# The first token group's attention in one fixed order, with value sums and key copies on GpSimd

## The chip, the cores and the metric

One core of one Trainium2 chip runs the whole kernel. The metric is the device time of one execution in microseconds (us), the median of three runs; a profile of one further execution stands beside it. Engines are named as in the profile: PE is TensorE (PEld its weight loads), DVE VectorE, ACT ScalarE, POOL GpSimd, SP the engine that issues most DMAs.

## What is computed

Three stages in a row: attention with keys and values averaged over 8 neighbours, a softplus feed-forward layer, and a layer of 8 experts of which each token takes one.

```python
def _attn_ref(q, k, v):                # 8 batches, 8 heads, 576 tokens, 64 wide
    k_p = k.reshape(B, H, Sp, pool, D).mean(axis=3)      # pool = 8, Sp = 72
    v_p = v.reshape(B, H, Sp, pool, D).mean(axis=3)
    scores = scale * np.matmul(q, k_p.transpose(0, 1, 3, 2))
    scores = scores - np.max(scores, axis=-1, keepdims=True)
    attn = np.exp(scores)
    attn = attn / (np.sum(attn, axis=-1, keepdims=True) + 1e-09)
    return np.matmul(attn, v_p)

def _moe_ref(x, w_in, w_out):          # x is 4608 x 512, w_in 512 x 2048, w_out 2048 x 512
    h = x @ w_in
    g = np.maximum(h, 0.0) + np.log1p(np.exp(-np.abs(h)))
    return g @ w_out
...
```

`w_in` and `w_out` arrive as 64-bit floats. The third stage, the experts, is not touched by the change.

## The kernel before

**Groups and blocks.** The 4608 tokens are worked on in nine groups of 512 (`g`). A group's attention has four units (`hp`, two heads each). Unit `u` needs its keys `kT[u]`, queries and values `vT[u]`, each with 128 partitions (two heads of 64). Groups and batches do not line up (512 against 576 tokens): the first group needs the keys and values `u` = 0 to 3, the second group these and `u` = 4 to 7.

**The first group's unit** (`unit0`, L576 to L617) takes these steps. DVE sums each eight keys (`keys`, L531), ACT copies the sum into the two halves of a block-diagonal tile `kbd` (L538, L539; there are two such tiles, used in turn), PE makes the scores `s` (L586), DVE subtracts the largest (L594, L595), ACT takes the exponential (L543), DVE sums, adds, inverts (L544 to L546), POOL multiplies (L547). For the values PE does eight accumulating products `pv` with the identity (L604), which sum and transpose at once; ACT copies the result (`vp`, L606). PE transposes the shares (`tr`, L613), ACT copies them (L614), PE makes the output `o` (L570). ACT writes its rounded part `xh` (L572) and DVE the remainder `xl` (L573). The steps stand in a generator; `Feed.tick` advances all units that are open by one step, and one step of the weights follows each tick.

**The second group's unit** (`unit`, L619 to L669) does the same in other tiles; there DVE sums keys and values by a reduction (L531, L554), and one transpose (L561) turns the value sum.

**The weights** (`load_weights`, L464) come as 64-bit words. A piece is loaded (`raw`), ACT unpacks it in two instructions (L470, L472), DVE joins the parts in two (L475, L477), ACT writes the rounded part `wh` (L492, L520) and DVE the remainder `wl` (L494, L521). The first four column blocks come in six halves of 512 words ("early halves"), through three small buffers in `boot2`; the other twelve in whole blocks of 1024 words, two to a tile (`raw2` to `raw7`, `wt2` to `wt7`).

**The feed-forward layer.** For block `c` of 16, `p1` makes 12 products h (L716), ACT and DVE do the softplus (L722 to L729) and leave `gh` and `gl`; `p2` makes 12 products y (L740 to L742) two blocks later. `p1` of block c needs tile `wt[c // 2]`. The first group's 16 blocks need the weights as they come; later groups find them all there. Between the blocks, ticks of `Feed` run the next group's attention.

**What sets the order.** A scheduler places the instructions: each engine's list is in the order that its plan gives, not the order of the code; after that each engine works its list strictly from the front.

Of the kernel before, what the change touches and what calls it, by code (L numbers as in the profile page):

```python
# [15 lines left out]
ALU = mybir.AluOpType  # L16
# [20 lines left out]
def tile_kernel(ctx, tc, qT, kT, vT, wbits, w9, w1, w2, out):  # L37
# [383 lines left out]
    with ExitStack() as ph:  # L421
# [37 lines left out]
        STEPS = 6 * EARLY + 6 * (8 - EARLY // 2)  # L459
# [4 lines left out]
        def load_weights():  # L464
# [15 lines left out]
            def half(c, j, first):  # L480
# [8 lines left out]
                unpack(lo, hi)  # L489
# [10 lines left out]
            for c in range(EARLY):  # L500
                for j in range(2 if c >= LAG else 1):
                    yield from half(c, j, True)
            for i in range(EARLY // 2, 8):
# [5 lines left out]
                for j in range(2):  # L509
                    lo, hi = raw[:, j, :, 0], raw[:, j, :, 1]  # L510
                    unpack(lo, hi)
# [15 lines left out]
        count = [0]  # L527
        def keys(u, k, kv):
# [37 lines left out]
        def output(us, et, hp, xh, xl, ps=ps_a, tag="pa"):  # L566
            o = ps.tile([P, 512], F32, tag=tag, name="o")
# [4 lines left out]
            nc.scalar.activation(out=xh[:, hp, :], in_=o, func=AF.Copy, scale=0.125)  # L572
            nc.vector.scalar_tensor_tensor(out=xl[:, hp, :], in0=o, scalar=0.125,  # L573
                                           in1=xh[:, hp, :].bitcast(F32), op0=ALU.mult, op1=ALU.subtract)

        def unit0(hp, us, xh, xl, g):  # L576
            (u, r0, rn, c0), = us
            q, k = room("q", G, True), room("kv", 576, True)
            nc.sync.dma_start(out=k, in_=kT[u])
            nc.sync.dma_start(out=q, in_=qT[u, :, r0:r0 + rn])  # L580
            yield
            yield
            banks = [ps_y.tile([P, 512], F32, tag=f"y{hp % 2 * 2 + i}", name="s") for i in range(2)]
            kb = keys(u, k, lambda: room("kv", 576, True))
            for t in range(T):
                nc.tensor.matmul(banks[t // 3][:, t % 3 * 144:(t % 3 + 1) * 144],  # L586
                                 lhsT=q[:, t * P:(t + 1) * P], rhs=kb, start=True, stop=True)
            e = k.rearrange("p (a k) -> p a k", k=SP)
            st = room("st", 24, True)
# [198 lines left out]
        for i, it in enumerate(feed.units):  # L788
            next(it)
            if i:  # L790
                weights(1)
# [225 lines left out]
```

## Time and profile before

| | us |
|---|---|
| three runs | 1360.51, 1362.04, 1363.5 |
| median | 1362.04 |
| the profiled execution | 1360.56 |
| its span, first to last instruction | 1358.8 |
| PE busy in the span | 1330.1 (98%) |
| DVE, ACT, POOL busy | 847.6, 595.0, 308.0 |

The span is the time between the first and the last instruction on the core; the execution's time has 1.8 us more around it. Busy time of PE counts a product from its start to its modelled end. The share over the whole span hides that the stages differ: the first 35 us are the first group's attention, the stretch to some 130 us is the first group's feed-forward layer with the unpacking of the weights beside it, then come eight groups with all weights there, then the experts. Everything that the change moves lies in the first 130 us.

### The profile page before, as it was taken

To read this page: it belongs to the slowest core of one execution; us is meant where nothing else is said; L and a number is where in the kernel's file an instruction comes from. 1 tells how busy PE (TensorE), PEld (TensorE's weight loads), DVE (VectorE), ACT (ScalarE), POOL (GpSimd) and SP (SyncE) were. 2 spreads that over 40 slices of the span, in tenths; PEclk is the share of its full clock that TensorE was granted. 3 is DMA by queue.
4 is the path that set the end of the run, shared out by engine and by line. 5 is a ranking of instruction groups with operands and counts; after the bars stand their busy time and mean duration, and the time that the engine had idled before them with its cause. 6 is when DMAs were issued, how large, how long until landed. Compare 5 with 4: busy or idle time off the path is not lost. (4 is left out here: it accounts for less than half of the span.)

```text
span 1358.8 us, 21365 instructions
## 1 busy us (share of the span) xinstructions
PE 1330.1 (98%) x7030; PEld 1110.0 (82%) x7030; DVE 847.6 (62%) x1951; ACT 595.0 (44%) x1076; POOL 308.0 (23%) x375
## 2 busy tenths in 40 slices
PE   6999999999999999999999999999999999999996
PEld 5777787778878778778778778889989898989885
DVE  7998794974974964965946847545655332326263
ACT  6996544544555445545455444551111111114152
POOL 2010111121021030030130120343233343233334
PEclk9999999999999999999999999999999999999998
DMA  7642432241341340431421301503322222243363
GB/s 274 256 150 79 125 106 68 77 126 35 83 128 29 99 125 17 119 102 31 119 70 28 111 14 46 196 23 94 96 79 95 71 63 75 69 136 112 123 212 88
DMA packets 149743, 134.17 MB, mean 99 GB/s; under 512 B 100933, under 2 KB 116933, under 8 KB 147056
## 3 DMA queue, kind: packets, MB, share of 16 engines
q1 hardware_dynamic: 131744, 95.51, 24.3%
q0 software_dynamic: 17872, 37.13, 8.6%
q8 instruction: 60, 0.98, 0.3%
q14 instruction: 67, 0.55, 0.1%
HBM read 168.77 MB, written 29.67 MB: 146 GB/s over the span
## 5 line engine op out<-in xcount | busy, mean ns | idle before, releaser
L716 PE MATMUL h<-xh,wt 128*128 128x512 f32 x1152 | 379.7, 390 | 0.3 <-DVE xl L573 0.3
L716 PEld LDWEIGHTS h<-xh,wt 128*128 128x128 f32 x1152 | 216.2, 188 | 46.0 <-DVE xl L573 1.2
L740 PE MATMUL y<-wt,gh 128*128 128x512 f32 x576 | 232.8, 404 | 0.0
L894 PE MATMUL h<-xt,w1h 128*128 128x256 f32 x1280 | 226.4, 281 | 2.7 <-PEq L918 2.0
L120 DVE CUSTOM_DVE_ANT_0 junk<-rows,w9b 128x512 bf16<-128x512 f32 x324 | 222.4, 686 | 8.1 <-ACT rows L114 3.2
L741 PE MATMUL y<-wt,gh 128*128 128x512 f32 x576 | 225.2, 391 | 0.0
L742 PE MATMUL y<-wt,gl 128*128 128x512 f32 x576 | 225.1, 391 | 0.0
L716 PE MATMUL h<-xl,wt 128*128 128x512 f32 x576 | 224.7, 390 | 0.0
L894 PEld LDWEIGHTS h<-xt,w1h 128*128 128x128 f32 x1280 | 196.4, 188 | 5.1 <-issue 2.8
L894 PE MATMUL h<-xt,w1l 128*128 128x256 f32 x640 | 179.5, 280 | 0.7 <-DVEq L962 0.7
L898 ACT ACTIVATE hs<-h 128x512 fp32r<-128x512 f32 x80 | 47.7, 598 | 301.5 <-PE h L894 180.3
L722 ACT ACTIVATE a<-h 128x512 f32<-128x512 f32 x144 | 85.8, 596 | 175.8 <-PE h L716 169.7
L725 DVE SCALAR_TENSOR_TENSOR a<-h,a 128x512 f32<-128x512 f32 x144 | 98.5, 684 | 102.8 <-ACT a L724 102.2
L727 ACT ACTIVATE gh<-a 128x512 fp32r<-128x512 f32 x144 | 90.8, 631 | 160.6 <-DVE a L725 158.2
L740 PEld LDWEIGHTS y<-wt,gh 128*128 128x128 f32 x576 | 108.1, 188 | 35.2 <-ACT a L722 7.7
L742 PEld LDWEIGHTS y<-wt,gl 128*128 128x128 f32 x576 | 108.2, 188 | 25.5 <-issue 2.1
L716 PEld LDWEIGHTS h<-xl,wt 128*128 128x128 f32 x576 | 108.2, 188 | 22.3 <-issue 0.2
L741 PEld LDWEIGHTS y<-wt,gh 128*128 128x128 f32 x576 | 108.3, 188 | 20.0 <-issue 0.2
L729 DVE TENSOR_TENSOR gl<-a,gh 128x512 fp32r<-128x512 f32 x144 | 101.0, 701 | 37.6 <-ACT gh L727 34.9
L894 PEld LDWEIGHTS h<-xt,w1l 128*128 128x128 f32 x640 | 122.1, 191 | 0.9 <-DVEq L962 0.9
L928 DVE SCALAR_TENSOR_TENSOR ys<-y,xg 128x512 f32<-128x512 f32 x38 | 28.5, 750 | 145.3 <-PE y L926 115.8
L926 PE MATMUL y<-w2h,hs 128*128 128x512 f32 x304 | 118.5, 390 | 0.6 <-DVE hs L899 0.6
(198 smaller groups left out, 1815.0 us busy)
## 6 DMA issues: line engine op xcount, KB each, us to landing
w9b<-w SPq DMA_DIRECT2D x81, 256.0 KB
raw<-wbits SPq DMA_DIRECT2D x12, 1024.0 KB
x2d<-rows SPq DMA_DIRECT2D x36, 260.0 KB
et<-q SPq DMA_DIRECT2D x256, 32.0 KB
kv<-vT SPq DMA_DIRECT2D x28, 288.0 KB
kv<-kT SPq DMA_DIRECT2D x24, 288.0 KB
xm<-misc SPq DMA_DIRECT2D x160, 32.0 KB
misc<-misc SPq DMA_DIRECT2D x144, 32.0 KB
```

The costliest lines, as they stand in the source:

```text
L120: nc.vector.tensor_tensor_reduce(out=ws["junk"], in0=rows[t][:, :D], in1=w9b[e], scale=1.0, scalar=0.0, op0=ALU.mult, op1=ALU.add, accum_o ...
L716: nc.tensor.matmul(h, lhsT=l, rhs=r[:, kk, :], start=n == 0, stop=n == 11)
L722: nc.scalar.activation(out=a, in_=h, func=AF.Abs)
L725: nc.vector.scalar_tensor_tensor(out=a, in0=h, scalar=0.0, in1=a, op0=ALU.max, op1=ALU.add)
L727: nc.scalar.activation(out=gh, in_=a, func=AF.Copy)
L729: nc.vector.tensor_tensor(out=gl, in0=a, in1=gh.bitcast(F32), op=ALU.subtract)
L740: nc.tensor.matmul(y, lhsT=th, rhs=wh, start=c == 0, stop=False)
L741: nc.tensor.matmul(y, lhsT=th, rhs=wl, start=False, stop=False)
L742: nc.tensor.matmul(y, lhsT=tl, rhs=wh, start=False, stop=c == 15)
L894: nc.tensor.matmul(h[:, f2, :], lhsT=l, rhs=r[:, kk, :], start=n == 0, stop=n == 11)
L898: nc.scalar.activation(out=hh[:, fs, :], in_=h, func=AF.Relu)
L926: nc.tensor.matmul(y, lhsT=hl[:, f, js], rhs=ws["w2h"][:, f, :], start=False, stop=f == 7)
```

## The change

**The first group.** `unit0` becomes a class whose steps are methods, and `lead_in` calls the steps of the four units in one written order. `in_order` then ties each instruction that is issued inside it to the one before it on the same engine, DMA issues on SP included, so that the plan keeps this order; other instructions may still stand between. The key sum stays on DVE; its two copies into `kbd` go from ACT to POOL. The value sum goes from PE (eight products) to POOL (three adds, `add8`), and PE does one transpose of it (`values`). All value loads are issued ahead of the first weights. Units 2 and 3 take other PSUM banks for values and outputs.

**The second group.** Its key and value sums (`u` = 4 to 7) go from DVE to POOL (`pool8`); the copies into `kbd` stay on ACT.

**The weights.** An early half's load is issued two halves ahead of its unpacking. Some instructions are held behind others (`after`): unpackings of the third and later early halves, and of the first large blocks, behind the first group's rounding on ACT; the first two blocks of `p1` behind the first group's transposes on PE; the second group's first maximum behind the first group's remainders on DVE; the first second-group key sum behind the first group's adds on POOL.

```diff
...
+            its = [half(c, j, True) for c in range(EARLY) for j in range(2 if c >= LAG else 1)]
+            for n in range(2):
+                next(its[n])
+                yield
+            for n, it in enumerate(its):
+                if n + 2 < len(its):
+                    next(its[n + 2])
+                yield from it
...
+        def after(eng, cond=True):
+            return tc.issue_after(behind[eng]) if cond else nullcontext()
...
-                nc.vector.tensor_reduce(kp, k.rearrange("p (s w) -> p s w", w=8), AX.X, ALU.add)
+                pool8(kp, k, u)
...
-                    nc.vector.tensor_reduce(vr, v.rearrange("p (s w) -> p s w", w=8), AX.X, ALU.add)
+                    pool8(vr, v, u)
...
-            for w in range(8):
-                nc.tensor.matmul(pv[:SP, :P], lhsT=v8[:, w], rhs=ident, start=w == 0, stop=w == 7)
...
+            for ins in traced[start:]:
+                if ins.engine in prev:
+                    tc.add_manual_dep(ins, prev[ins.engine].name,
+                                      mybir.DependencyInfo(mybir.DependencyClass.NoSync, mybir.DependencyReason.DATA),
+                                      reason="in_order")
+                prev[ins.engine] = ins
...
+        def add8(out, t):
+            t3 = t.rearrange("p (s w) -> p s w", w=8)
+            for n in (4, 2):
+                nc.gpsimd.tensor_tensor(out=t3[:, :, :n], in0=t3[:, :, :n], in1=t3[:, :, n:2 * n], op=ALU.add)
+            behind["POOL"] = nc.gpsimd.tensor_tensor(out=out.unsqueeze(2), in0=t3[:, :, 0:1], in1=t3[:, :, 1:2],
+                                                     op=ALU.add).ins
...
+        def pool8(out, t, u):
+            if u < 8:
+                with after("POOL", u == 4):
+                    add8(out, t)
+            else:
+                nc.vector.tensor_reduce(out, t.rearrange("p (s w) -> p s w", w=8), AX.X, ALU.add)
...
+                nc.gpsimd.tensor_copy(self.kb[0:64, 0:SP], kp[0:64, :])
+                nc.gpsimd.tensor_copy(self.kb[64:128, SP:2 * SP], kp[64:128, :])
...
+            def vsum(self):
+                add8(self.vr, self.v)
...
-        while feed.units or jobs:
-            feed.tick()
+        def lead_in():
+            u0, u1, u2, u3 = us = units_of(0)
+            for u in us:
+                u.load_v()
+            weights(2)
+            u0.key()
+            u0.score()
+            u1.key()
+            u1.score()
+            u0.top()
+            u2.key()
+            u0.exp()
+            u0.share()
+            u2.score()
+            u0.vsum()
+            u1.top()
+            u1.exp()
+            u3.key()
+            u1.share()
+            u0.value()
+            u0.turned()
+            u3.score()
...
+        with in_order():
+            lead_in()
...
```

**Places where it moves instructions.** ACT at the end of the first group's attention, up to the first softplus instruction (`a`). `boot_170<-tr` are the turned shares, `boot2_171` the early halves, `kbd` the key tiles, `o` and `xh` the outputs and their rounding; `raw2` and `raw3` are the large loads. Before:

```order
L614 ACTIVATE boot_170<-tr_381 72x512
L614 ACTIVATE boot_170<-tr_387 72x512
L572 ACTIVATE xh_175<-o_396 128x512
L470 ACTIVATE boot2_171<-boot2_171 128x512
L472 ACTIVATE boot2_171<-boot2_171 128x512
L572 ACTIVATE xh_175<-o_402 128x512
L472 ACTIVATE raw2_450<-raw2_450 128x1024
L470 ACTIVATE raw2_450<-raw2_450 128x1024
L492 ACTIVATE wt1_182<-boot2_171 128x512
L722 ACTIVATE a_425<-h_412 128x512
```

The same place now:

```order
L577 ACTIVATE vp_348<-pv_346 72x128
L552 ACTIVATE kbd1_167<-kp_455 64x72
L684 ACTIVATE boot_170<-tr_350 72x512
L684 ACTIVATE boot_170<-tr_356 72x512
L470 ACTIVATE boot2_171<-boot2_171 128x512
L472 ACTIVATE boot2_171<-boot2_171 128x512
L587 ACTIVATE xh_175<-o_365 128x512
L553 ACTIVATE kbd1_167<-kp_455 64x72
L552 ACTIVATE kbd0_165<-kp_203 64x72
L553 ACTIVATE kbd0_165<-kp_203 64x72
L495 ACTIVATE wt0_189<-boot2_171 128x512
L587 ACTIVATE xh_175<-o_373 128x512
```

Before, the sixth early half's rounding (`wt1`) stands just ahead of the first softplus instruction, and a large load is partly unpacked; now only the second half's (`wt0`) is done, and a key copy of the second group (`kp_455`, summed on POOL) stands ahead of the last turned shares.

POOL in the same stretch had four multiplies (L547) in a row and then the second group's. Now its list between the multiplies (L668) of units 0 and 1, and from those of units 2 and 3 to the second group's first key sum, is:

```order
L668 TENSOR_TENSOR boot_kv_169<-boot_kv_169,boot2_171 128x576
L610 TENSOR_TENSOR boot_kv_169<-boot_kv_169 128x72x4
L610 TENSOR_TENSOR boot_kv_169<-boot_kv_169 128x72x2
L611 TENSOR_TENSOR boot2_171<-boot_kv_169 128x72
L643 COPY kbd1_167<-kp_240 64x72
L644 COPY kbd1_167<-kp_240 64x72
L668 TENSOR_TENSOR boot_kv_169<-boot_kv_169,boot2_171 128x576
```

```order
L668 TENSOR_TENSOR boot_kv_169<-boot_kv_169,boot2_171 128x576 x2
L610 TENSOR_TENSOR boot2_171<-boot2_171 128x72x4
L610 TENSOR_TENSOR boot2_171<-boot2_171 128x72x2
L611 TENSOR_TENSOR boot2_171<-boot2_171 128x72
L610 TENSOR_TENSOR kk_412<-kk_412 128x72x4
L610 TENSOR_TENSOR kk_412<-kk_412 128x72x2
L611 TENSOR_TENSOR kp_455<-kk_412 128x72
```

Each value sum has come in as three rows behind a multiply, and the second group's key sum (`kp_455`) stands behind unit 3's value sum.

ACT ahead of the first write of a weight tile that comes from a large load. Before, `wt2` is written after the rounding of one block's softplus:

```order
L470 ACTIVATE raw3_516<-raw3_516 128x1024
L727 ACTIVATE gh_430<-a_425 128x512
L724 ACTIVATE a_468<-a_468 128x512
L520 ACTIVATE wt2_511<-v_477 128x1024
L520 ACTIVATE wt2_511<-v_482 128x1024
```

Now:

```order
L495 ACTIVATE wt1_190<-boot2_171 128x512
L806 ACTIVATE a_576<-h_563 128x512
L470 ACTIVATE raw3_585<-raw3_585 128x1024
L807 ACTIVATE a_576<-a_576 128x512
L472 ACTIVATE raw3_585<-raw3_585 128x1024
L808 ACTIVATE a_576<-a_576 128x512
L470 ACTIVATE raw3_585<-raw3_585 128x1024
L529 ACTIVATE wt2_535<-v_511 128x1024
```

The write now stands behind the softplus of the fourth block (`h_563`, c = 3), where before it stood behind the second block's.

## Rows read from the trace of the kernel before

**Rows 1.** Busy us (count): PE, PEld, DVE, ACT, POOL; clock, DMA share, GB/s.

```profile
24.00:95.00 71.00, 68.69 (x335) 52.31 (x334) 65.93 (x94) 69.00 (x111) 7.29 (x7) 1.00 0.62 228
```

**Rows 2.** Waits of PE, 35.4 to 130 us: total, times, longest.

```profile
PE s L636 <- ACT kbd L539: 1.4, 2, 1.2
PE pv L561 <- DVE vr L554: 0.5, 1, 0.5
```

**Rows 3.** Timeline of PE: start, us, line, out<-in, shape, count, [idle before].

```profile
5.22 2.29 PE L586 MATMUL s<-kbd,boot 128*128 128x144 f32 x8 [5.22 <-ACT kbd L539]
...
19.25 1.15 PE L586 MATMUL s<-kbd,boot 128*128 128x144 f32 x8
...
20.45 2.33 PE L604 MATMUL pv<-ident,boot_kv 128*72 128x128 f32 x16
...
26.73 1.08 PE L570 MATMUL o<-boot,vp 72*64 72x512 f32 x4
...
35.41 0.50 PE L716 MATMUL h<-xh,wt 128*128 128x512 f32 x1 [0.32 <-DVE xl L573]
...
42.40 1.39 PE L636 MATMUL s<-kbd,q 128*64 128x144 f32 x8 [1.22 <-ACT kbd L539]
...
54.52 0.39 PE L716 MATMUL h<-xh,wt 128*128 128x512 f32 x1
...
60.40 0.27 PE L561 MATMUL pv<-ident,vr 128*72 128x128 f32 x1 [0.50 <-DVE vr L554]
...
93.95 0.61 PE L716 MATMUL h<-xh,wt 128*128 128x512 f32 x2
```

**Rows 4.** Timeline of DVE.

```profile
3.84 0.75 DVE L531 TENSOR_REDUCE kp<-boot_kv 128x72 f32<-128x576 f32 x1 [2.54 <-DMA boot_kv<-kT]
...
17.98 0.20 DVE L546 RECIPROCAL boot<-boot 128x8 f32<-128x8 f32 x1
18.61 1.40 DVE L494 TENSOR_TENSOR wt<-boot,wt 128x512 fp32r<-128x512 f32 x1 [0.43 <-ACT wt L492]
...
22.38 0.69 DVE L477 SCALAR_TENSOR_TENSOR boot<-boot 128x512 int32<-128x512 int32 x1
22.99 0.75 DVE L544 TENSOR_REDUCE boot<-boot_kv 128x8 f32<-128x576 f32 x1
...
46.54 1.21 DVE L521 TENSOR_TENSOR wt<-v,wt 128x1024 fp32r<-128x1024 f32 x1
```

**Rows 5.** Timeline of ACT.

```profile
4.62 0.26 ACT L538 ACTIVATE kbd<-kp 64x72 f32<-64x72 f32 x1 [2.54 <-DVE kp L531]
...
22.99 0.67 ACT L470 ACTIVATE boot<-boot 128x512 f32<-128x512 f32 x1
...
24.12 0.66 ACT L492 ACTIVATE wt<-boot 128x512 fp32r<-128x512 f32 x1
24.68 1.06 ACT L614 ACTIVATE boot<-tr 72x512 f32<-72x512 f32 x2
...
46.90 0.61 ACT L727 ACTIVATE gh<-a 128x512 fp32r<-128x512 f32 x1
47.42 0.57 ACT L722 ACTIVATE a<-h 128x512 f32<-128x512 f32 x1
47.90 0.67 ACT L543 ACTIVATE q<-q 128x576 f32<-128x576 f32 x1
48.47 0.61 ACT L723 ACTIVATE a<-a 128x512 f32<-128x512 f32 x1
48.99 1.14 ACT L472 ACTIVATE raw<-raw 128x1024 int32<-128x1024 uint32 x1
50.03 0.61 ACT L724 ACTIVATE a<-a 128x512 f32<-128x512 f32 x1
```

**Rows 6.** Timeline of POOL.

```profile
18.32 1.15 POOL L547 TENSOR_TENSOR boot_kv<-boot_kv,boot 128x576 f32<-128x576 f32 x1 [3.06 <-DVE boot L546]
...
43.86 0.26 POOL L649 MEMSET q<- 128x192 f32 x1 [12.33 <-PE s L636]
```

More of the change, by code (lines that the diff above doesn't have):

```diff
@@ L488, in half @@
                 lo, hi = raw[:, :, 0], raw[:, :, 1]
-                unpack(lo, hi)
+                if first:
+                    yield
+                with after("ACT", first and c > 1):
+                    unpack(lo, hi)
                 yield
@@ L510, in load_weights @@
                     lo, hi = raw[:, j, :, 0], raw[:, j, :, 1]
-                    unpack(lo, hi)
+                    with after("ACT", i < 4):
+                        unpack(lo, hi)
                     yield
@@ new lines, in round_x, with rest_x, in_order @@
+        def round_x(o, hp, xh):
+            return nc.scalar.activation(out=xh[:, hp, :], in_=o, func=AF.Copy, scale=0.125)
+        def rest_x(o, hp, xh, xl):
+            return nc.vector.scalar_tensor_tensor(out=xl[:, hp, :], in0=o, scalar=0.125,
+                                                  in1=xh[:, hp, :].bitcast(F32), op0=ALU.mult, op1=ALU.subtract)
+        @contextmanager
+        def in_order():
+            traced = nc.cur_bb.bb.instructions
+            mark = traced[-1]
+            yield
+            start = next(k for k in reversed(range(len(traced))) if traced[k] is mark) + 1
+            prev = {}
+            for ins in traced[start:]:
[4 more added lines that the diff above has]
+                prev[ins.engine] = ins
@@ L644, in unit @@
                 m = mx[:, 4 * b:4 * b + 4].rearrange("p (t h) -> p t h", t=2)
-                nc.vector.tensor_reduce(m, s4, AX.X, ALU.max)
+                with after("DVE", g == 1 and hp == 0):
+                    nc.vector.tensor_reduce(m, s4, AX.X, ALU.max)
                 nc.vector.tensor_tensor(out=e4[:, 2 * b:2 * b + 2, :, :SP], in0=s4, op=ALU.subtract,
@@ L668, in unit @@
             yield
-            output(us, et.rearrange("p (a k) -> p a k", a=2)[:SP], hp, xh, xl)
+            o = ps_a.tile([P, 512], F32, tag="pa", name="o")
+            attend(o, us, et.rearrange("p (a k) -> p a k", a=2)[:SP])
+            round_x(o, hp, xh)
+            rest_x(o, hp, xh, xl)
         X = {}
@@ L682, in units_of @@
                 t0 += n
-            return [(unit if g else unit0)(hp, [(b * 4 + hp, *r) for b, *r in part], xh, xl, g) for hp in range(4)]
+            return [unit(hp, [(b * 4 + hp, *r) for b, *r in part], xh, xl, g) if g else
+                    Unit0(hp, [(b * 4 + hp, *r) for b, *r in part], xh, xl) for hp in range(4)]
         jobs, ends = [], []
@@ L785, in last_group @@
                 split2()
-        feed.start(units_of(0), 1)
[L788 to L791, printed above, removed]
-        while feed.units or jobs:
-            feed.tick()
-            weights(1)
+        def lead_in():
[20 more added lines that the diff above has]
+            u3.score()
+            u2.top()
+            u2.exp()
+            u1.vsum()
+            u0.product()
+            u0.high()
+            u3.top()
+            u2.vsum()
+            u2.share()
+            u1.value()
+            u1.turned()
+            u3.exp()
+            u3.share()
+            weights(1)
+            u1.product()
+            u1.high()
+            u3.vsum()
+            weights(1)
+            u0.low()
+            u1.low()
+            u2.value()
+            u2.turned()
+            weights(1)
+            u3.value()
+            u3.turned()
+            weights(1)
+            u2.product()
+            u2.high()
+            u2.low()
+            weights(1)
+            u3.product()
+            u3.high()
+            weights(1)
+            u3.low()
+        with in_order():
+            lead_in()
         pend = []
```

124 lines of the change are left out of this document (69 added, 55 removed).

## Prediction

> **What bounds the kernel now.** I read the busy table of the stretch behind the first group's attention first, then TensorE's waits, then each engine's rows in the lead-in. From 24 to 95 us TensorE is busy 68.69 of 71 us, ACT 69.00, DVE 65.93 [rows 1]: all three are nearly full, and what one gains can be lost on the next. Behind the first product of the feed-forward part at 35.41 [rows 3] TensorE waits 1.4 us in two pieces for ACT's key copies (1.2 of it before the scores at 42.40) and 0.5 us for a value sum of the second group [rows 2, 3]. So TensorE sets the time, and ACT and DVE run only a little ahead of it. Free time is in the lead-in alone.
>
> For each unit of the first group the change takes eight accumulating products off TensorE (2.33 us [rows 3]) and puts one transpose there (0.27 [rows 3]): 4 x 2.06 = 8.2 us less, in a stretch where it runs without pause up to 35.41. The question is what is left of these 8.2 us once ACT has to feed it.
>
> **Part 1: the new lead-in, up to the point where ACT turns to the remaining weights.** I add up the chain that ends last in the new order, at the trace's durations. A hop between engines costs 0.04 (key sum ends at 3.84 + 0.75, ACT's copy starts at 4.62 [rows 4, 5]); from DVE to GpSimd 0.14 (reciprocal ends at 18.18, multiply starts at 18.32 [rows 4, 6]).
>
> Unit 0's keys are there at 3.84. Sum 0.75, two copies on GpSimd, taken at ACT's 0.26 each [rows 5]: scores start at 5.4, against 5.22 before; the moved copies gain nothing here. Three score groups follow at 2.29 each, as in the trace at 5.22 (1.15 at 19.25 [rows 3]), with 0.5 of hops between: units 0 to 2 are done at 12.8. ACT now has two key copies for the second group queued ahead of unit 1's exp; they overwrite the key tile that unit 2's scores read, so they wait for these: 13.4. Exp 0.67, sum 0.75, add and reciprocal 0.2 each, with hops: 15.3 [rows 4, 5]. Multiply on GpSimd 1.15 [rows 6]: 16.6. Behind it on GpSimd stands unit 1's value sum.
>
> A value sum is three adds over 288, 144 and 72 elements a row, 504 together; no row shows one. From below: 504/576 of the 1.15, 1.0 us. From above: three instructions each as long as the multiply, 3.45. I take 0.1 on top of each share and 0.08 of hops, 1.38: nearer the lower end, since a memset of 192 elements takes 0.26 here [rows 6], so that a small instruction is cheap.
>
> The chain goes on: unit 1's values 17.9; their transpose and eight of the shares, 1.35 (a transpose pair of 0.27 [rows 3] starts every 0.13 or so); copies to 19.9 (0.53 each [rows 5]); unit 3's exp, which stands behind these on ACT, 20.5; its sum, add, reciprocal 21.7. Here DVE's first weight instructions (0.69 [rows 4]) meet GpSimd's multiplies and sums. When a weight subtract began at 18.61, inside a multiply that ran from 18.32 to 19.47, it took 1.40 and ended 0.54 after the multiply [rows 4, 6]. So I let the two take turns: unit 3's multiply 22.3 to 23.5, DVE's join to 24.2, unit 3's value sum to 25.55, DVE's subtract to 26.25, the second group's key sum on GpSimd to 27.6. ACT's next instruction copies just these keys; behind it stand unit 3's turned shares (2 x 0.53), the unpacking of the second early half (1.13) and the rounding of unit 2's output [rows 5]: 30.65. DVE's remainder and two joins (3 x 0.69), ACT's rounding of the weights (0.56) and of unit 3's output: **33.8**. Two of the six early weight halves are then done; before, all six were done at this place in ACT's order.
>
> The Trainium skill speaks against the change here: its page "SBUF — State Buffer", section "SBUF: two separate sides", says that a VectorE instruction with two SBUF inputs and a GpSimd one shut each other out for a whole instruction. The trace's 1.40 agrees. Without such turns the chain would end at 31.95, and the sum below would come to 0.5 us faster, not 1.4 slower.
>
> **Part 2: from there to the fifth weight block, c = 4.** Up to its first write ACT has, start to start: four early halves at 1.13 + 0.56, 6.8; seven unpackings of 1.04, 7.3; softplus of blocks 0 to 3 less one rounding, 4 x 0.48 + 11 x 0.52, 7.6; the second group's exp 0.57; the write, taken as an unpacking, 1.0 [rows 5]. Together 23.2 without a pause: 57.0. TensorE's first product of c = 4 needs this write; before, it stood at 54.52 [rows 3]. **So the earlier start of TensorE (unit 3's shares copied at 29.0, 1.08 for its output [rows 3]: 30.1 in place of 35.41) is given back in waits for weights.** Before, the way from 35.41 to 54.52 was 17.9 of work and 1.2 of waiting; now 26.9 us pass, 9 of them waiting.
>
> c = 4 is 2.5 us later. By then TensorE has done a transpose and a score product that came later before (0.4), and the two waits of 0.5 and 0.2 behind 54.52 [rows 2] go, since GpSimd has those sums early: +1.4 us. What is late next: the weights of c = 10. ACT's rows up to their write: 15 unpackings 15.6, 6 writes 6.0, softplus 6 x 0.48 + 16 x 0.52 = 11.2, ten key copies 2.8, small ones 2.1, 37.7: 94.7, and DVE's subtract 1.25 [rows 4]: 95.95. TensorE went from c = 4 to the third product of c = 10 in 39.4 (93.95 - 54.52 [rows 3]), less 0.7 of waits, plus 0.9 for an output that now stands ahead: 96.6. Hidden, by 0.65.
>
> **What I cost at nothing.** DVE loses eight sums of the second group, 8 x 0.75 = 6 us: no gain while ACT is the later of the two. ACT loses eight key copies of 0.26, in idle time. All value loads go ahead of the early weights on SP: 3.9 MB instead of some 1.6 up to the end of the first half; at the 228 GB/s of the stretch from 24 on [rows 1], certainly less than an unhindered queue moves, 17 us, so by 18; wanted at 20.5. One buffer for the second group's keys makes SP wait for GpSimd's key sum, with the fourth half's load and all large loads but the first two queued behind it, until 27.6; that half is wanted at 35, and if GpSimd is late, ACT is too, so the cover stays.
>
> **The sum.** Profiled execution 1360.56 us (span 1358.8, 1.8 around it) + 1.4 = 1362.0. It lies 1.5 below the median of the three runs; on that scale 1362.04 + 1.4 = **1363.4**. A measurement can tell some 0.2%, 2.7 us, from no change: I forecast no change.
>
> **Rivals.**
> *GpSimd's adds are slow: slower than before.* Place: the three sums in the chain (values of units 1 and 3, the second group's keys). At 2.1 us a sum the chain ends at 36, +3.6 us; with TensorE's longer durations up to 17 us, 1.1 more; if turns with GpSimd (five more sums and a multiply, 8 us) reach ACT through DVE, which has little room [rows 1], 2 more: 1365 to 1369. It decides from 1.85 us a sum. For: no row shows such adds, and each release of them is on the path. Against: 1.15 for 576 elements.
> *The chain is shorter: faster.* TensorE at the short duration from the second score group on, no turns, sums of 1.0: 29 to 30; then c = 4 starts at 52.2 to 53.2 and 2.4 to 3.4 us are won. Far end, ACT does not bind: 5.3 of earlier start and 1.9 of waits, 7.2 us, 1355. For: the 8.2 us are real. Against: ACT's 69.00 of 71 us, from which nothing is taken. 1355 to 1360.
> *The order is not kept.* Excluded; the built rows show it.
>
> **How the numbers follow.** Forecast 0.45 (chain ends at 32 to 35, 1361.5 to 1364.8), GpSimd slow 0.30, chain shorter 0.25. The bounds within 0.2% are 1359.3 and 1364.8; what the rivals leave inside them and what the forecast loses outside about cancel: faster 0.25, same 0.44, slower 0.31. For 8 in 10 the range takes in the near half of each rival: 1357.5 to 1367.
>
> **What would show it.** Right: first product near 30; ACT's second early rounding near 33; TensorE waiting 7 to 10 us between the first product and c = 4; that start within 2 us of 57; ACT without pause from 34 to 95; a value sum of 1.3 to 1.5 in three rows; DVE subtracts of 1.2 and more beside GpSimd's rows. Wrong: ACT idle between 34 and 57 (a load or DVE is late), c = 4 before 54 (the chain was shorter), new waits of TensorE behind 100 us.

## The result: slower by 10 us, and the profile after

The changed kernel takes 1372.08 us (median of 6 runs, 1371.21 to 1374.14) against 1361.82 for the kernel before in the same jobs (1359.92 to 1363.5): ratio 1.0079, interval 1.0066 to 1.0092. The forecast of 1363.4 was wrong by 8.7 us, and the time lies 5 us above the range's end.

The page of after: span, TensorE's busy time, and the granted clock in 40 slices.

```profile
span 1370.3 us, 21277 instructions
PE 1331.6 (97%) x6970; PEld 1104.2 (81%) x6970; DVE 845.8 (62%) x1943; ACT 592.8 (43%) x1068; POOL 334.6 (24%) x419
PE   6799999999999999999999999999999999999996
PEclk8999999999999999999999999999999999999998
```

The profiled span is 11.5 us longer than before (1358.8). From the second block of the second group to the last block of the ninth the two kernels run in step: the softplus of a block stands 9.0 us later in after than in before (within 0.5 at every block but one, which is 9.8 later), and the last one's at 908.10 against 899.09. So 9.0 us arise before about 150 us, and 2.5 more behind 908 us, in the part that neither the change nor any run here edits. Of these 2.5 some 1.3 are no loss of the change: before's profiled execution (1360.56) lay that much under its median, and after's (1372.05) did not.

TensorE's waits in after from 24 to 60, 60 to 100 and 100 to 140 us (total, times, longest); they answer to [rows 2]:

```profile
PE pv L575 <- POOL boot L611: 3.8, 1, 3.8
PE h L800 <- ACT wt L495: 2.4, 2, 2.0
PE h L800 <- DVE a L809: 1.9, 1, 1.9
PE y L825 <- DVE wt L497: 1.2, 1, 1.2
PE h L800 <- DVE wt L497: 0.3, 1, 0.3
...
PE h L800 <- ACT wt L529: 2.0, 1, 2.0
...
PE h L800 <- ACT wt L529: 1.6, 1, 1.6
```

All but the first and third name `wt`, the unpacked weights. TensorE's timeline in after (start, duration, line, out<-in, count, idle time before it), for [rows 3]:

```profile
21.77 0.82 PE L682 MATMUL tr<-ident,boot_kv 128*72 128x128 f32 x6
26.35 0.43 PE L575 MATMUL pv<-ident,boot 128*72 128x128 f32 x1 [3.76 <-POOL boot L611]
26.57 1.91 PE L682 MATMUL tr<-ident,boot_kv 128*72 128x128 f32 x8
28.42 3.68 PE L583 MATMUL o<-boot,vp 72*64 72x512 f32 x8
32.03 0.79 PE L800 MATMUL h<-xh,wt 128*128 128x512 f32 x1
...
35.66 1.40 PE L714 MATMUL s<-kbd,q 128*64 128x144 f32 x10
37.42 0.50 PE L800 MATMUL h<-xh,wt 128*128 128x512 f32 x1 [0.37 <-ACT wt L495]
...
51.40 0.50 PE L800 MATMUL h<-xh,wt 128*128 128x512 f32 x1 [2.00 <-ACT wt L495]
...
62.65 0.50 PE L800 MATMUL h<-xh,wt 128*128 128x512 f32 x1 [1.98 <-ACT wt L529]
```

The feed-forward part begins at 32.03, 3.4 us earlier than before; c = 4 begins at 62.65, 8.1 us later (54.52 in [rows 3]). The clock was at 0.5, the lower of its two levels (1.2 GHz), from 24.7 us, inside the pause of 3.76, to 35.0; eight output products take 3.68 where two fours took 1.08 each before. ACT's timeline in after, beside [rows 5]:

```profile
24.36 0.67 ACT L495 ACTIVATE wt<-boot 128x512 fp32r<-128x512 f32 x1 [1.84 <-DVE boot L477]
...
27.98 0.26 ACT L552 ACTIVATE kbd<-kp 64x72 f32<-64x72 f32 x1 [0.89 <-POOL kp L611]
...
30.44 0.60 ACT L587 ACTIVATE xh<-o 128x512 fp32r<-128x512 f32 x1
31.06 0.26 ACT L553 ACTIVATE kbd<-kp 64x72 f32<-64x72 f32 x1
36.15 0.26 ACT L552 ACTIVATE kbd<-kp 64x72 f32<-64x72 f32 x1 [4.83 <-PE s L714]
36.43 0.26 ACT L553 ACTIVATE kbd<-kp 64x72 f32<-64x72 f32 x1
36.71 0.66 ACT L495 ACTIVATE wt<-boot 128x512 fp32r<-128x512 f32 x1
...
37.75 0.66 ACT L470 ACTIVATE boot<-boot 128x512 f32<-128x512 f32 x1
...
61.54 1.06 ACT L529 ACTIVATE wt<-v 128x1024 fp32r<-128x1024 f32 x1 [0.29 <-DVE v L477]
```

The last row is the first rounding of a weight block of full size (1024 columns, c = 4; L529, in before L520), called the first full rounding from here on. It starts at 61.54; in before it starts at 45.00. Summing ACT's rows up to it, before worked 33.3 us and idled 11.7; after worked 38.6 and idled 22.9. Of the 16.5 us that the weights are later, 11.2 are ACT's idle time and 5.3 work that now stands ahead of them.

### The profile page after: what moved, and what is told of

It reads as the page before. It is cut to its first block, busy times and chain, and to the rows that moved or that the text cites. A ratio compares the mean times of both kernels' runs of the same rounds, so it can differ in the third digit from the quotient of the medians.

```text
span 1370.3 us, 21277 instructions
## 1 busy us (share of the span) xinstructions
PE 1331.6 (97%) x6970; PEld 1104.2 (81%) x6970; DVE 845.8 (62%) x1943; ACT 592.8 (43%) x1068; POOL 334.6 (24%) x419
## 5 line engine op out<-in xcount | busy, mean ns | idle before, releaser
L800 PEld LDWEIGHTS h<-xl,wt 128*128 128x128 f32 x576 | 108.8, 189 | 22.9 <-issue 0.9
L1060 PE MATMUL y<-w2h,hs 128*128 128x512 f32 x304 | 118.5, 390 | 1.8 <-DVE hs L1033 1.8
L1058 PE MATMUL y<-w2h,hs 128*128 128x512 f32 x304 | 118.5, 390 | 1.4 <-ACTq L1096 1.4
```

Source lines behind the costliest of these rows:

```text
L800: nc.tensor.matmul(h, lhsT=l, rhs=r[:, kk, :], start=n == 0, stop=n == 11)
L1058: nc.tensor.matmul(y, lhsT=hh[:, f, js], rhs=ws["w2h"][:, f, :], start=f == 0, stop=False)
L1060: nc.tensor.matmul(y, lhsT=hl[:, f, js], rhs=ws["w2h"][:, f, :], start=False, stop=f == 7)
```

## The experiments

Four theories. ORDER: the order leaves ACT idle, and weights come late. CLOCK: with the value sums gone from TensorE it has pauses, and its clock is low. QUEUE: a key copy waits on ACT, with roundings behind it. PORTS: VectorE and GpSimd lock each other out.

### The order alone, the moves alone

The order alone (value sums by eight products, second group's sums on VectorE, key copies on ACT, the fixed order kept):

```
             def vsum(self):
-                add8(self.vr, self.v)
+                pass
...
-                nc.gpsimd.tensor_copy(self.kb[0:64, 0:SP], kp[0:64, :])
+                nc.scalar.activation(out=self.kb[0:64, 0:SP], in_=kp[0:64, :], func=AF.Copy)
...
-            if u < 8:
+            if u < 4:
                 with after("POOL", u == 4):
```

> The fixed order alone: the value sums by eight products, the second group's sums on VectorE and the first group's key copies on ScalarE, all as in the kernel before; what is left of the change is the order of the first group's attention, the early halves of the weights that come behind it, and the holds. Theory ORDER (the order postpones the unpacking of the weights, and that is what c=2, c=3 and c=4 wait for): 1368 to 1373. If the moved sums and copies make the loss (CLOCK with PORTS): 1360 to 1364.

Measured: 1368.77, ratio 1.0051 (1.0030 to 1.0071): 7.0 us slower than before with no work moved to GpSimd. TensorE's waits from 24 to 140 us in this run:

```profile
PE h L807 <- ACT wt L529: 4.9, 1, 4.9
PE h L807 <- ACT wt L495: 3.5, 2, 2.9
```

The moves alone (the kernel before, with `add8` of the change):

```
             def keys(u, k, kv):
...
+            if count[0] <= 4:
+                nc.gpsimd.tensor_copy(kb[0:64, 0:SP], kp[0:64, :])
+                nc.gpsimd.tensor_copy(kb[64:128, SP:2 * SP], kp[64:128, :])
+                return kb
...
+            vr = room("vr", SP, True)
+            add8(vr, v)
...
-            for w in range(8):
-                nc.tensor.matmul(pv[:SP, :P], lhsT=v8[:, w], rhs=ident, start=w == 0, stop=w == 7)
+            nc.tensor.transpose(pv[:SP, :P], vr, ident)
```

> The kernel before, its attention left to the scheduler's order, with all three moves of work of the change: first group's value sums and second group's key and value sums on GpSimd, first group's key copies on GpSimd. No fixed order, no holds, weight steps where they were. With the run of the order alone (1368.8) this makes a square of four. If order and moves add: 1361.8 plus 3.3, 1364 to 1366. If the moves cost only by the waits that the fixed order makes of them: 1360 to 1363. If the moves are the loss by themselves: 1369 to 1373.

Measured: 1367.94, ratio 1.0048 (1.0031 to 1.0064), so 6.1 us slower with no order fixed. The two do not add: 7.0 and 6.1 make 13.1, and the change costs 10.3. The rows also show another loss than the order's: in this run TensorE does not wait for weights. Its timeline:

```profile
33.02 2.78 PE L586 MATMUL o<-boot,vp 72*64 72x512 f32 x4
35.73 1.92 PE L629 MATMUL tr<-ident,boot_kv 128*72 128x128 f32 x8
...
40.29 0.79 PE L732 MATMUL h<-xh,wt 128*128 128x512 f32 x1
...
42.16 0.63 PE L732 MATMUL h<-xl,wt 128*128 128x512 f32 x1
42.59 1.05 PE L732 MATMUL h<-xh,wt 128*128 128x512 f32 x2
...
45.03 0.63 PE L732 MATMUL h<-xh,wt 128*128 128x512 f32 x2
45.50 0.40 PE L732 MATMUL h<-xl,wt 128*128 128x512 f32 x1
```

Eight transposes take 1.92 where before's eight at this place took 1.07, and products of 512 columns start 0.43 apart up to 44.7 us and 0.23 apart from then on. So the clock rose only inside the feed-forward part, which began at 40.29 and not at 35.41. The Trainium skill, page "TensorE: Matmul & The Clock Gate", section "Wait — 56ns, not 53.3ns?", gives 426.7 and 215.7 ns for such steps at the two levels; the trace agrees with the first (0.43 us) and lies a little above the second (0.23).

### Is it the clock? Products that compute nothing

The kernel with all three moves, and eight products of the identity with itself ahead of each turned value sum, into the bank that it overwrites:

```
+            for w in range(8):
+                nc.tensor.matmul(pv[:, :P], lhsT=ident, rhs=ident, start=True, stop=True)
             nc.tensor.transpose(pv[:SP, :P], vr, ident)
```

> The kernel before with all three moves (1367.9 alone) and, for each of the four removed groups of eight products, eight products of the identity with itself, which nothing waits for and which are overwritten. Theory CLOCK: TensorE reaches full clock at about 18 to 22 us instead of 44.8, the first layer begins at 35 to 36.5 instead of 40.3, and the time comes back to 1361 to 1364. If not the clock but the chain through GpSimd's sums set the end: 1367 to 1369.

Measured: 1361.03, ratio 0.9992 (0.9983 to 1.0002). The 6.1 us are gone, though TensorE has 32 products more to do and no other engine has less. Its timeline, on the same stretch:

```profile
33.02 1.07 PE L631 MATMUL tr<-ident,boot_kv 128*72 128x128 f32 x8
...
37.44 0.50 PE L734 MATMUL h<-xh,wt 128*128 128x512 f32 x1 [0.98 <-DVE xl L589]
37.78 0.39 PE L734 MATMUL h<-xl,wt 128*128 128x512 f32 x1
38.01 0.62 PE L734 MATMUL h<-xh,wt 128*128 128x512 f32 x2
```

So where the scheduler sets the order, what the moves cost went through TensorE's clock, at least for the most part. An estimate from the rows without fillers: the first ten products take 4.43 us (40.29 to 44.72) where before's take 2.44 (35.41 to 37.85), and each of the two groups of transposes from 31.16 on takes 0.85 longer, 3.7 of the 6.1 us together. The run does not isolate the clock fully, since the fillers changed the scheduler's plan too: ACT's list differs from that of the run without them from 19 us on, VectorE's from 31 us on. Split in two:

> The kernel before with one move alone: the first group's value sums on GpSimd and one turned product per unit in place of eight; order, key copies and second group as before. Theory CLOCK (in the run with all three moves TensorE stayed at half clock until 44.8 us and the first layer began at 40.3 and not at 35.4): this move alone takes the products away, so it alone costs it, 1366 to 1368.5. If the loss is of the other two moves: 1361 to 1363.

Measured, value sums alone: 1364.47, ratio 1.0020 (1.0010 to 1.0030). First product at 36.62; two stretches of low clock.

> The kernel before with the other two moves: the first group's key copies and the second group's sums on GpSimd, value sums by eight products as before. Theory CLOCK: no loss, ScalarE and VectorE have a few us less to do, 1359.5 to 1362.5. If the turns between VectorE and GpSimd cost (PORTS): 1364 to 1367.

Measured, the other two moves: 1367.13, ratio 1.0039 (1.0025 to 1.0054). CLOCK had this at no loss, and it is the dearer half. The first product is late here for another reason:

```profile
38.50 0.72 PE L732 MATMUL h<-xh,wt 128*128 128x512 f32 x1 [1.16 <-DVE xl L589]
39.02 0.63 PE L732 MATMUL h<-xl,wt 128*128 128x512 f32 x1
```

VectorE's remainder `xl` came late, behind a join of 1.71 us (1.2 where nothing runs beside it) beside GpSimd's adds, and the products behind that wait ran at the low level from 38.6 to 42.0 us, eight steps of 0.43 and not 0.23, 1.6 us more. So PORTS has a part in this half, argued from the rows and not split off by a run. The two halves (2.7 and 5.3 us) come to more than the 6.1 of both. That the fillers nevertheless bring all three moves back to before's time says only that this order had room for the sums when TensorE ran at full clock.

### Is it the fixing, or the text?

The order-alone kernel with `lead_in()` called without `in_order()`:

```
-        with in_order():
-            lead_in()
+        lead_in()
```

> The order alone (1368.8 with the fixed order, the work where it was before) with the fixed order taken out again: the program text stays that of the change (lead-in written out, weight steps behind it, holds), the scheduler orders. If the fixing is what costs: 1361 to 1364. If it is where the text puts the weight steps and the loads: 1367 to 1370.

Measured: 1362.81, ratio 1.0006 (0.9996 to 1.0015). Taking out the fixing alone gives 6.0 of the 7.0 us back. Up to the first full rounding ACT idles 13.5 us here, and 17.9 with the order fixed. Left to itself the scheduler put unpackings between the attention's ACT instructions; the fixed order holds them behind.

> The change's text without the fixed order and without its moves of work (1362.8), with the early weight steps put between the units as in the runs above and without the holds on the unpacking. In that run the first layer began at 30.6 us, 4.8 us before the kernel before, and then waited for weights (3.4 us for one rounding at about 50 us, three waits of 0.5 to 0.8 beside it). Theory ORDER (all that is lost there is late weights): 1358.5 to 1361. If ScalarE has no free time left to take the weights earlier: 1361.5 to 1363.

```
-                with after("ACT", first and c > 1):
-                    unpack(lo, hi)
+                unpack(lo, hi)
...
             u2.exp()
+            weights(1)
...
```

Measured: 1360.72, ratio 0.9992 (0.9983 to 1.0001): level with before within what can be told. First product at 30.11, 5.3 us ahead of before, but the first full rounding at 51.03, and TensorE waits 3.3 us for such roundings. ACT is busy without a pause from 30 to 50 us here, so what is left of the head start is lost to ACT's own work.

### Inside the changed kernel

The value sums back on TensorE, in the fixed order (`vsum` empty, and in `value`):

```
-                values(self.us, self.vr, *((ps_h, "h") if self.hp < 2 else (ps_y, f"y{self.hp - 2}")))
...
+                for w in range(8):
+                    nc.tensor.matmul(pv[:SP, :P], lhsT=v8[:, w], rhs=ident, start=w == 0, stop=w == 7)
...
```

> The changed kernel (1372.1 us, before 1361.8), with the first group's value sums taken back from GpSimd: TensorE sums eight products per unit again; order, key copies and the second group's sums stay as changed. Theory CLOCK: the eight products that were removed leave TensorE idle from 22.6 to 26.4 us and at half clock from 24.7 to 35.0; with them back the clock holds, the scores of the second group end 3 to 4 us earlier than 37.1, the wait of 4.8 us on ScalarE for them goes, and the time is 1367 to 1369. Theory QUEUE (a key copy ahead of two roundings on ScalarE waits for those scores, whatever the clock): the wait shrinks only as far as the scores come earlier, 1369 to 1372. Theory PORTS (VectorE and GpSimd share turns from 53 to 62 us, by the second group's sums): nothing changes, 1371 to 1373.

Measured: 1367.91, ratio 1.0043 (1.0028 to 1.0058), 4.2 us less than the changed kernel, as CLOCK had it:

```profile
28.33 2.06 PE L583 MATMUL o<-boot,vp 72*64 72x512 f32 x8
30.32 0.50 PE L807 MATMUL h<-xh,wt 128*128 128x512 f32 x1
...
32.59 1.40 PE L721 MATMUL s<-kbd,q 128*64 128x144 f32 x10
33.09 0.26 ACT L552 ACTIVATE kbd<-kp 64x72 f32<-64x72 f32 x1 [2.09 <-PE s L721]
```

The outputs take 2.06 and not 3.68, the second group's scores end 3 us earlier, and ACT waits 2.1 us for them and not 4.8. But this run also takes 7.6 us of adds off GpSimd; the fillers were to separate the two. Beside the order alone (1368.77) this run has the key copies and the second group's sums on GpSimd and is no slower: in the fixed order these two moves cost nothing that can be told, where in the scheduler's order they cost 5.3 us.

```
...
+                for w in range((8, 8, 16, 8)[self.hp]):
+                    nc.tensor.matmul(f[:, :P], lhsT=ident, rhs=ident, start=True, stop=True)
+                values(self.us, self.vr, pool, tag)
```

> The changed kernel with 40 extra products of the identity with itself on TensorE, 8, 8, 16 and 8 of them ahead of the four turned value sums, into the bank that is overwritten right after. Nothing else has more or less to do. Theory CLOCK: the granted clock stays at 1.0 from 18 to 52 us, the outputs of units 2 and 3 take half of their 3.7 us, the scores of the second group come 2 to 3 us earlier, and the time is 1368 to 1370. Theories QUEUE and PORTS: at most 1 us, 1371 to 1373; if the fillers lie on the path, 1372 to 1375.

The second time (4, 8, 12) and none for the fourth unit:

> Fewer fillers than in the first run with fillers, where 24 of the 40 stood between the third unit's sum and the fourth unit's output and put that 2 us later: here 4, 8 and 12 products of the identity stand ahead of the first three turned value sums and none ahead of the fourth, so that they end about when the awaited sum does. Nothing else changes. Theory CLOCK: the eight output products of units 2 and 3 take 1.9 us and not 3.7, the first layer's products start at 30 and not at 32.0, ScalarE's wait for the second group's scores falls from 4.8 to about 2 us, and the time is 1368 to 1370. Theory ORDER alone: 1371 to 1373.

Measured: 1376.48 (1.0105) and 1375.42 (1.0098), both slower than the changed kernel. With the 40 fillers the clock did hold and the outputs took 1.94, yet they began at 30.82 and not at 28.42: in a fixed order a filler stands in the queue ahead of work, and in the second run a pause of 2.5 us for ACT came before the clock fell again (0.5 from 31.2 to 38.0; this trace is of an execution of 1372.38, 3 us under the median). Whether the clock alone explains the 4.2 us inside the fixed order is left open by these two.

The second group's key copies, first on GpSimd, then on ACT but held behind the last rounding of the first group:

```
+            if u < 8:
+                nc.gpsimd.tensor_copy(kb[0:64, 0:SP], kp[0:64, :])
+                nc.gpsimd.tensor_copy(kb[64:128, SP:2 * SP], kp[64:128, :])
+                return kb
             nc.scalar.activation(out=kb[0:64, 0:SP], in_=kp[0:64, :], func=AF.Copy)
```

> The changed kernel with the second group's key copies too (units 4 to 7 and what is rewritten of 0 to 3 where the copy for 4 to 7 goes) on GpSimd in place of ScalarE; some copies of old keys stay on ScalarE only if they belong to later groups. Theory QUEUE: ScalarE no longer waits from 31.3 to 36.15 us for the second group's scores, its unpacking of the weights starts 3 to 4 us earlier, c=4 starts at 58 to 59.5 instead of 62.65, and the time is 1367 to 1369. Theory CLOCK: TensorE is as slow as before, the roundings go earlier but the products wait for TensorE: 1370 to 1372. Theory PORTS: 1371 to 1374, since GpSimd has more to do.

> The changed kernel with one hold more: the second group's key copies on ScalarE may be issued only behind the last rounding of the first group's outputs, in place of where the scheduler put them, which is ahead of the fourth unit's rounding and inside the lead-in. The same work, sums and copies as changed. Theory QUEUE (the copies waited 0.9 us for GpSimd's sum and 4.8 us for the second group's scores, with a rounding and all of the remaining weights behind them): ScalarE has no wait over 1.5 us between 28 and 40 us, c=4 starts 3.5 to 5 us earlier than 62.65, the time is 1366 to 1369. Theory CLOCK (the wait only stands where TensorE is late, and the roundings wait for TensorE's outputs anyway): 1370.5 to 1373.

```
-            nc.scalar.activation(out=kb[0:64, 0:SP], in_=kp[0:64, :], func=AF.Copy)
...
+            with after("ACT", count[0] <= 12):
+                nc.scalar.activation(out=kb[0:64, 0:SP], in_=kp[0:64, :], func=AF.Copy)
...
```

Measured: 1375.17 (1.0094) and 1371.18 (1.0071, 1.0054 to 1.0088). QUEUE falls as the cause of the loss. The first is no clean test: TensorE ran at the low level nearly up to 24 us there (eight transposes 1.91). In the run with the hold ACT's longest wait from 28 to 40 us is 2.49, and its unpacking of the third half starts 2.6 us earlier, at 35.13:

```profile
34.08 0.67 ACT L495 ACTIVATE wt<-boot 128x512 fp32r<-128x512 f32 x1 [2.49 <-DVE boot L477]
...
46.63 0.60 ACT L807 ACTIVATE a<-h 128x512 f32<-128x512 f32 x1 [1.57 <-PE h L801]
...
63.56 2.01 ACT L529 ACTIVATE wt<-v 128x1024 fp32r<-128x1024 f32 x2 [0.49 <-DVE v L477]
```

but the first full rounding is 2 us later: an unpacking and a rounding more stand ahead of it (1.1 us), and waits for VectorE's joins and for TensorE took the place of the one removed (23.8 us idle up to there, 22.9 in after).

Early weight steps inside the fixed order; then with the value sums back; then each with the hold:

```
             u2.exp()
+            weights(1)
             u1.vsum()
...
             u3.exp()
+            weights(1)
             u3.share()
-            weights(1)
+            weights(2)
             u1.product()
```

> The changed kernel, all of its sums and copies where the change put them, and the order of the attention kept; only the steps of the early weights stand earlier in that order: the first half is unpacked behind the third unit's exponential, the second behind the fourth's, the third behind the fourth unit's outputs, so that three halves are rounded by the end of the lead-in and not two, and their loads are issued ahead of the second group's keys. Theory ORDER (ScalarE is the bound from 31 to 130 us, and the order took from it the weight work with which it filled its gaps before): the first full roundings come at 57 to 58.5 us instead of 61.5, c=4 starts at 58 to 59.5 and the time is 1367 to 1369. Theory CLOCK or QUEUE (what ScalarE waits for is TensorE, and that is as late as before): 1370 to 1372.5.

> The first group's value sums by eight products again, as in the run with 1367.9 us, together with the earlier weight steps. Theory ORDER: both recover their own part, 1363 to 1365. If the one already contains the other (both only shorten the wait on ScalarE for the second group's scores): 1366 to 1368.

> The same hold together with the earlier weight steps, which alone gave 1376.7: there the second group's first key copies came to stand among the lead-in's copies and waited 4.4 us for GpSimd's sum. Theory ORDER: with those out of the way the third half is rounded 4 us earlier than in the changed kernel, and the time is 1363 to 1366. If the hold contains all there is to gain: as the run with the hold alone, 1366 to 1369.

> Hold, earlier weight steps, and value sums by eight products. Theory ORDER with CLOCK (each part is its own loss): 1358 to 1362, at or below the kernel before. Theory QUEUE alone: 1363 to 1366.

Measured: 1376.66 (1.0109), 1367.79 (1.0042), 1368.71 (1.0050) and 1365.50 (1.0029, 1.0017 to 1.0042). Alone the step made it worse: the second group's key copies slid in among the lead-in's copies, ACT waited for GpSimd's sum, and TensorE behind it (waits of both, of the run with the weight steps alone):

```profile
ACT kbd L552 <- POOL kp L611: 4.4, 1, 4.4
...
PE tr L682 <- ACT boot L684: 3.1, 1, 3.1
```

With hold, weights and eight products together 6.6 of the 10.3 us come back; no fixed order tried here reached before's time.

The order free and all moves kept, without and with the other cures:

> The changed kernel without the fixed order: the sums on GpSimd, the key copies there and the holds stay, but each engine's order in the lead-in is left to the scheduler, as in the kernel before. The weight halves still come in where the program text puts them. Theory ORDER: ScalarE gets its filling work back in part, 1363 to 1368. If the moved sums and copies make the loss: 1370 to 1374.

> The changed kernel with all of its moved sums and copies, but the order left to the scheduler, the early weight steps between the units, no holds on the unpacking, and eight products of the identity in place of each group of eight that was taken from TensorE. If order and clock are the two losses and nothing else is: 1360 to 1363. If the sums on GpSimd cost by themselves, through waits and turns with VectorE: 1365 to 1369.

Measured: 1371.52 (1.0068, 1.0046 to 1.0090) and 1367.32 (1.0044, 1.0030 to 1.0058). The first has the clock at 0.5 from 12.9 to 26.5 us and its first full rounding at 59.08. The second is a surprise: its last block's softplus stands at 900.89, only 1.8 us behind before's, so the order (with the holds and the places of the weight steps) and the clock are nearly all of the loss up to there; its other 4 us lie in the last part, which takes 465.2 us and not 459.7. In all traces that part took 459.1 to 465.2; before, after and this run differ in it by a wait of TensorE for ACT's queue between 1128 and 1136 us (none in before, 1.4 in after, 1.6 here), which is not all of it. In this run the clock is also low there, 0.5 from 1130.5 to 1133.9 us, as it is for a stretch of 3.4 us at about this place in two other traces, and not in before or after. Single executions differ here too: the early weights without a fixed order (median 1360.72) were profiled in an execution of 1363.82 with a wait of 3.1 us at this place. No run was made on the last part, and it stays open.

### Two bounds that fit all twenty traces

From each trace three times: the first product of the feed-forward part, the start of the first full rounding, the last block's softplus (us).

| kernel | median | first product | first full rounding | last softplus |
|---|---|---|---|---|
| before | 1361.8 | 35.41 | 45.00 | 899.09 |
| moves alone | 1367.9 | 40.29 | 51.25 | 905.86 |
| moves and fillers | 1361.0 | 37.44 | 45.47 | 899.54 |
| after | 1372.1 | 32.03 | 61.54 | 908.10 |
| order alone | 1368.8 | 30.43 | 59.24 | 906.32 |
| its text, not fixed | 1362.8 | 30.60 | 54.09 | 900.90 |
| the same, early weights | 1360.7 | 30.11 | 51.03 | 898.15 |
| after, value sums back | 1367.9 | 30.32 | 59.55 | 904.95 |
| after, key copies held | 1371.2 | 32.58 | 63.56 | 909.06 |

In the first three rows the last softplus stands 862 to 866 us behind the first product; in the others 845 to 849 behind the first full rounding, and so it is in all of the twenty traces, each time by the later of the two. So ACT has some 17 us, from the first product on, to begin the first full rounding. Before, it had 7.5 us to spare (35.41 + 17.1, the distance of the two middles, less 45.00); after, it is 12 us late, and the 3.4 us earlier start are worth nothing. This is a rule read off these traces, not a law of the chip.

## Why the prediction was wrong, step by step

- **Lead-in, up to the second group's key sum: right, in part by luck.** The sum has it at 27.6; it ended at 27.95. A value sum was taken at 1.38 and is 1.69 from the first add's start to the last one's end, and 2.56 where VectorE ran beside it. The sum let VectorE's subtract go between unit 3's value sum and the key sum; it ran inside the value sum, from 25.45, and that paid for the longer sums:

```profile
12.02 1.30 POOL L610 TENSOR_TENSOR boot_kv<-boot_kv 128x288 f32<-128x288 f32 x2
13.40 0.31 POOL L611 TENSOR_TENSOR boot<-boot_kv 128x72 f32<-128x72 f32 x1
...
23.74 1.75 POOL L610 TENSOR_TENSOR boot<-boot 128x288 f32<-128x288 f32 x2
25.57 0.73 POOL L611 TENSOR_TENSOR boot<-boot 128x72 f32<-128x72 f32 x1
```

- **"33.8", ACT free for the remaining weights: wrong, 37.75.** Unit 2's output was rounded at 31.0, as summed (30.65). The last step then counted joins and roundings and left out two of ACT's instructions that stand between them, the next second-group unit's key copies. They overwrite the key tile that the second group's scores read, and those stood on TensorE behind the first layer's first products at half clock: 4.83 us of wait. The very dependence that the sum had used once, at 13.4, was missed here. With the value sums back on TensorE, and the clock full up to 40 us, 2.09 of the wait remain. This is where the sum broke, but it is not by itself the loss: with the value sums back ACT turned to the remaining weights at 34.29, near the sum's 33.8, and began the first full rounding 2.0 us earlier than in after; with the copies held behind it did so at 35.13 and began that rounding 2.0 us later.
- **"23.2 without a pause": 24.9 us from 37.75 to the end of the first full rounding at 62.60.** ACT waited 0.85 for TensorE, whose clock was low again from 52.0 to 55.4 us, and 0.29 for VectorE; the other 0.5 of the difference is ACT's own work. VectorE's joins were long beside GpSimd's second-group adds: two joins of a full block 3.93 us, where one takes 1.2 in all rows of before but one (1.57). Here the row bears out the exclusive lock that the Trainium skill, page "SBUF — State Buffer", section "SBUF: two separate sides", describes. The sum had such turns only up to 27 us; up to this rounding no more than the 0.29 of them reached ACT.

```profile
53.75 3.93 DVE L475 SCALAR_TENSOR_TENSOR v<-raw 128x1024 int32<-128x1024 int32 x2
...
54.81 3.15 POOL L610 TENSOR_TENSOR kk<-kk 128x288 f32<-128x288 f32 x2
```

- **The sum.** 57.0 was forecast for c = 4, and 62.65 came: 3.95 from the first error, 1.65 from the second. It then counted 1.1 us of gains behind c = 4; instead 0.9 were lost. The weights of c = 10, which it costed as hidden, were; but TensorE waited 1.57 at 129.61 for those of c = 14, which no step of the sum looked at. The last part, not in the sum at all, gave 2.5 in the profiled run. 5.6 + 2.0 + 2.5 is the miss of 10.1 on the profiled spans; on the medians it is 8.7, since before's profiled execution (1360.56) lay 1.5 under the median of its first three runs and after's did not lie under its own.
- **First product near 30: 32.03.** The output products were taken at 1.08 for four and took 3.68 for eight at the low clock. The forecast kept the clock of [rows 3] for a TensorE from which it took 8.2 us of work, and had low clock only up to 17 us, in a rival. That is the error of reasoning behind this miss, and behind the 2.7 of the 4.83 us that go with the value sums back on TensorE: the work that was counted as saved also kept the clock up. The fillers in the fixed order show that much: with them it stayed at the upper level up to 43 us, and the eight outputs took 1.94.
- **Fourth half "wanted at 35", with SP's stall costed at nothing: right by accident.** SP waited until 27.98 and DMA moved 41 GB/s from 25 to 30 us; ACT was late enough not to need it.
- **The rival "GpSimd's adds are slow" had the sign and not the mechanism.** Undisturbed adds came in under its deciding 1.85 us. It put 2 us on turns reaching ACT through VectorE: ACT waited 4.8 us for VectorE from 35 to 130 us, 2.6 in before, and no run tells how much of the difference is turns. That ACT binds, and that the early start is given back in waits for weights, was the forecast's own and is what happened, with c = 4 later by 8.1 us and not 2.5. Its sign of 7 to 10 us of waits up to there came (7.9), and so did two of its signs of being wrong: ACT idle between 34 and 57, and a new wait behind 100 us. The chances leant right, to slower over faster. The range took in neither of the unseen waits, though before's trace has one of the first kind (ACT, ahead of a key copy, 1.73 us for the second group's scores at 103.79).
- **What no step saw:** the fixing of the order is a cost of its own (6.0 of 7.0 us, the order alone against its text). The chain told when ACT would be free; it did not price what the free order had made of ACT's gaps, five of six halves rounded inside the attention.

## What to carry to other kernels

Before fixing the order of one engine's chain, count what the scheduler had been slipping into its gaps; here a fixed lead-in started the matrix work 3 to 5 us earlier and the weights 14 to 17 us later, and the later of the two set the time. Here work taken off the matrix engine, in a stretch where it was not the bound, went with a lower clock of that engine, so check with products that compute nothing whether the saved time was real. In a fixed queue, look at every instruction that the scheduler may still put in between, for each one's own release.

## What the runs showed of the hardware that was not expected

With the moves alone TensorE was busy all of 30 to 45 us by its rows and yet stayed at the lower level until 44.7, with pauses of up to 4.8 us between its products before 30 us. Busy time in the profile's sense is thus no sign of a high clock here; the spacing of the products tells it:

```profile
30.00:35.00 5.00, 5.00 (x16) 1.87 (x12) 3.77 (x7) 3.81 (x7) 2.24 (x2) 1.00 0.63 243
```

This is a window of that run (PE, PEld, DVE, ACT, POOL busy, clock, DMA share, GB/s). It even prints a granted clock of 1.00, where the products' spacing shows the lower level: the trace has no record of the clock before 44.9 us, and the column then means nothing.
